# A long-convolution block with a token-mixing MLP: work of the second layer norms moved from VectorE to GpSimd and ScalarE

## The chip, the cores and the metric

The kernel runs on one core of a Trainium2 chip. A core has TensorE (matrix products into PSUM), VectorE, ScalarE and GpSimd (elementwise work), and SyncE, whose queue issues most of the DMAs. Each engine takes its instructions in the order in which the program lists them; semaphores make one engine wait for another. The time is the device time of one execution in microseconds (us). Before the change it is 712.46 us, the median of three runs (706.91, 712.46 and 717.07).

In the profile, PE is TensorE, PEld its weight loads, DVE is VectorE, ACT is ScalarE, POOL is GpSimd and SP is SyncE. L60 is line 60 of the kernel; as all plain two-operand operations go through one helper on that line, they are told apart by their tiles.

## The reference

All tensors are float32; there are S = 2048 tokens, D = 640 channels and F = 1728 hidden units.

```
mod = silu(c) @ w_mod                      -> sa, ca, ga, sb, cb, gb   (640 each)
h   = layernorm(q) * (1 + ca) + sa
kv  = conv4(k, shift_k) * v                (causal, 4 taps, by channel)
y   = longconv(kv, ssm_k) + kv * ssm_D     (causal, 2048 taps, by channel; an FFT)
x   = q + ga * (h * y)
h2  = layernorm(x) * (1 + cb) + sb
u   = gelu(layernorm(h2)^T @ w1 + b1)      (over tokens: 640 x 1728)
out = x + gb * (u @ w2 + b2)^T
```

There are two layer norms in a row after the convolution: one over x, then, after scale and shift, one inside the MLP. Both are over the 640 channels of one token.

## The kernel before

The work has three stages. The first (to about 300 us) does the convolution by channel groups of 128 (NC = 5), with the Fourier transforms as matrix products (`step1`, `f2`, `i2`, `i1`). The third (from about 381 us) does the MLP: `w1` in 14 blocks of hidden units, then `w2`. The change lies between them and at the end of the first.

**Rows and pairs.** After the convolution the 2048 tokens lie as 16 rows `j` of 128 tokens by 640 channels, rows 0 to 7 in the tile `xa`, 8 to 15 in `xb`. They are handled in eight pairs `pr`. For a pair, the steps are:

- `gate` (L310) multiplies the convolution's result from PSUM by the gate, and adds it to x. For the last channel group it is called in parts: rows 0 and 1, rows 2 to 7, and rows 8 to 15 (`half` 1).
- `x1_stats` (L681), mean and variance of a row, on VectorE.
- `root_in` and `root` (L699, L710): 1/sqrt(variance + eps). GpSimd adds eps to the variance, ScalarE takes the square root, and VectorE makes it exact in a Newton step of four small instructions (`newton`, L326), the third of which multiplies by the variance plus eps. The list `roots` tells which rows' first norms and which rows' second norms share one root; there are nine, 0 to 8.
- `norm1` (L720), the first norm, on ScalarE.
- `second` (L724): VectorE multiplies by `CB` (1 + cb), sums, and adds `SB`; ScalarE squares and sums for the variance of the second norm.
- `halves` and `rests` (L740, L744): ScalarE writes the normalised row rounded to the matrix engine's format (the high part), VectorE writes what is left (the rest). They come one root later.
- `products` (L749): three matrix products (high by high, weight's rest by high, high by rest) for each row and block of hidden units, into four PSUM accumulators `acc[0..3]`: the first four blocks of the MLP.

**Weights.** A block of `w1` is split in the same way. For the first four blocks this is done by groups of four rows: `split_rows` (L416) makes the high parts on ScalarE (L419) and the rests on VectorE, one instruction of 128 x 512 for each block. Groups 0 and 1 are split at the end of the convolution (blocks 0, 1 and 3, and block 2 a little later, when its buffer is free), groups 2 and 3 in the loop over pairs, the high parts in pass 3 and 5, the rests in pass 4 and 6. From block 4 on `split_w` (L423) does whole blocks, in two buffers that blocks 0 and 1 leave.

**Modulation rows.** `mod_row` (L360) spreads a row of 640 numbers over the partitions by a product with ones into PSUM; `CB` is copied from there with 1 added (L380, VectorE), `SB` by ScalarE (L378).

**After the products.** `u_evac` (L844) applies gelu to an accumulator on ScalarE and splits it into high part and rest (ScalarE, VectorE). Four PSUM slots go round: block 4 takes the slot of `acc[0]`, so its products wait for `u_evac(0)`. ScalarE's first gelu loads another function table (at L847 in the profile).

The order on each engine is written out by hand; there is no scheduler. What stands in the text of the program first is issued first on its engine. GpSimd's queue holds, before the change, only the gate and convolution work of the first stage and then the small additions of `root_in`.

Of the kernel before, what the change touches and what calls it, by code (L numbers as in the profile page):

```python
# [10 lines left out]
F32R = mybir.dt.float32r  # L11
AF = mybir.ActivationFunctionType
ALU = mybir.AluOpType

S, D, F = 2048, 640, 1728
DC = 128
NC = D // DC
EPS = 1e-5
# [32 lines left out]
def mixer_kernel(ctx: ExitStack, tc: tile.TileContext, q, k, v, shift_k, ssm_k, ssm_D, w1, b1, w2, b2, c,  # L51
# [11 lines left out]
    def mem(tag, n, name=None):  # L63

        return sb.tile([128, n], F32, name=name or tag, tag=tag, bufs=1)
# [244 lines left out]
    def gate(c, ps, half, eng=pool, j0=0, j1=8, then=()):  # L310
        a = A1[:, 8 * half + j0:8 * half + j1]
        av = a.rearrange("p j (m e) -> p e j m", e=2)
        TT(dve, av, ps.rearrange("p (e j m) -> p e j m", e=2, j=8)[:, :, j0:j1], av, ALU.mult)
        for f_ in then:
            f_()
        x = XH[half][:, j0:j1, DC * c:DC * c + DC]
        TT(eng, x, x, a, ALU.add)
# [8 lines left out]
    def newton(r, t, v, n=None):  # L326

        dve.reciprocal(r, t)
        dve.scalar_tensor_tensor(t, r, -0.5, r, op0=ALU.mult, op1=ALU.mult)
        TT(dve, t, t, v, ALU.mult)  # L330
        dve.scalar_tensor_tensor(r, t, 1.5, r, op0=ALU.add, op1=ALU.mult)
# [28 lines left out]
    def mod_row(i, t, slot=None, later=False):  # L360

        ps, j = psum(slot).rearrange("p (h m) -> p h m", h=2), i % 3
        for h in range(2):
            pe.matmul(ps[:, h, 0:320], ones[32 * j:32 * j + 1, 0:1].to_broadcast([1, 128]),
                      t[32 * j:32 * j + 1, 320 * h:320 * h + 320], start=True, stop=True)
        ps = ps[:, :, 0:320]
        two = lambda t: t.rearrange("p (h m) -> p h m", h=2)
        if later:
            return lambda: act.activation(two(GB), ps, AF.Copy)
        if i == 0:  # L370
            act.activation(two(G0), ps, AF.Copy)
        elif i == 1:
            act.activation(two(G1), ps, AF.Copy, bias=1.0)
        elif i == 2:
            TT(dve, two(G0), ps, two(G0), ALU.mult)
            TT(dve, two(G1), ps, two(G1), ALU.mult)
        elif i == 3:
            act.activation(two(SB), ps, AF.Copy, accum_out=msb)  # L378
        elif i == 4:
            dve.tensor_scalar(two(CB), ps, 1.0, None, op0=ALU.add)  # L380


    NF, NW = 14, 4
# [12 lines left out]
    def load_w(i, t=X):  # L396
        if i >= NF + NW:
            return
        if i < NF:
            t = j16(t)  # L400
            for b in range(2):
                sync.dma_start(t[64 * b:64 * b + 64],
                               dram(w1, 16 * b * F + fo(i), [[32 * F, 64], [F, 16], [1, 128]]))
            raw[i] = (t, [slice(0, 8), slice(8, 16)])
        else:
            t = f14(t)
            load_w2(t, i - NF, 0, 14)
            raw[i] = (t, [slice(0, 7), slice(7, 14)])
# [7 lines left out]
    def split_rows(r, t, blocks, hi=True, lo=True):  # L416
        j, t = slice(4 * r, 4 * r + 4), t.rearrange("p (j m) -> p j m", j=4)
        for f in blocks if hi else ():
            act.activation(blk[f][0][:, j].bitcast(F32R), t[:, :, 128 * f:128 * f + 128], AF.Copy)  # L419
        for f in blocks if lo else ():  # L420
            TT(dve, blk[f][1][:, j].bitcast(F32R), t[:, :, 128 * f:128 * f + 128], blk[f][0][:, j], ALU.subtract)

    def split_w(i, t2=None, eng=dve):  # L423
        if i >= NF + NW:
            return
        if t2 is None:
            t2 = T_wb[i % 2]
        view = j16 if i < NF else f14
        hi, lo = view(t2[:, 0:2048]), view(t2[:, 2048:4096])
        t, parts = raw.pop(i)  # L430
        for f in parts:
            act.activation(hi[:, f].bitcast(F32R), t[:, f], AF.Copy)
        for f in parts:
            TT(eng, lo[:, f].bitcast(F32R), t[:, f], hi[:, f], ALU.subtract)
        blk[i] = hi, lo
# [243 lines left out]
    acc = []  # L679
# [4 lines left out]
            dve.bn_aggr(mv[:, j, :], bst[:, j])  # L684


    V_, T_, R_ = (T_kt[:, o:o + 32] for o in (1280, 1312, 1344))
    place = {}
    roots = (((), (0, 1)), ((0, 1), (2, 3)), ((2, 3), (4, 5)), ((4, 5), (6, 7, 8, 9)), ((6, 7), (10, 11)),
             ((8, 9), (12, 13)), ((10, 11), (14, 15)), ((12, 13), ()), ((14, 15), ()))  # L690
# [8 lines left out]
    def root_in(n):  # L699

        second_, first_ = roots[n]
        o = start[n]
        if second_:
            pool.tensor_scalar(V_[:, o:o + 2], V_[:, o:o + 2], 1 / D, EPS, op0=ALU.mult, op1=ALU.add)
            o += 2
        if first_:
            pool.tensor_scalar(V_[:, o:start[n + 1]], mv[:, first_[0]:first_[-1] + 1, 1], EPS, None, op0=ALU.add)
        act.activation(T_[:, start[n]:start[n + 1]], V_[:, start[n]:start[n + 1]], AF.Sqrt)

    def root(n):  # L710

        o = slice(start[n], start[n + 1])
        newton(R_[:, o], T_[:, o], V_[:, o])
        first_ = roots[n][1]
        if first_:
            f = slice(first_[0], first_[-1] + 1)
            dve.scalar_tensor_tensor(nm1[:, f], mv[:, f, 0], -1.0, R_[:, start[n + 1] - len(first_):start[n + 1]],
                                     op0=ALU.mult, op1=ALU.mult)

    def norm1(pr):  # L720
        for j in (2 * pr, 2 * pr + 1):
            act.activation(row(j), XR(j), AF.Identity, scale=at(R_, 1, j), bias=nm1[:, j:j + 1])
# [17 lines left out]
    def halves(pr):  # L740
        for j in (2 * pr, 2 * pr + 1):
            act.activation(H[j][0].bitcast(F32R), row(j), AF.Identity, scale=at(R_, 2, j))

    def rests(pr):  # L744
        for j in (2 * pr, 2 * pr + 1):
            dve.scalar_tensor_tensor(H[j][1].bitcast(F32R), row(j), at(R_, 2, j), H[j][0], op0=ALU.mult,
                                     op1=ALU.subtract)
# [46 lines left out]
    products(0, range(3))  # L794
    x1_stats(range(4, 6))
    second(1)
    gate(NC - 1, ps, 1, dve, then=(lambda: root_in(2), lambda: root(2), lambda: halves(1), lambda: norm1(2)))
    spill(NC - 1, (1,))
    products(0, [3])
    rests(1)  # L800
# [10 lines left out]
    for pr in range(3, 8):  # L811
        second(pr)
        if pr > 3:
            rests(pr - 1)
            products(pr - 1)
        if pr in (4, 6):
            split_rows(pr // 2, X if pr == 4 else P, range(4), False, True)
        if pr < 6:
            x1_stats(range(2 * pr + 4, 2 * pr + 6))
        root_in(pr + 1)  # L820
        root(pr + 1)
        halves(pr)
        if pr < 6:
            norm1(pr + 2)
        if pr in (3, 5):
            split_rows(pr // 2 + 1, X if pr == 3 else P, range(4), True, False)
        if pr == 4:
            load_w(4)
    rests(7)
    products(7)  # L830

# [60 lines left out]
        rest(3, a)  # L892

    T_wb = [mem("w0", 4096, "wb0b"), mem("w1", 4096, "wb1b")]
    split_w(4)
    load_w(5)
    for f_ in range(4):
        u_evac(f_, acc[f_])
    for f_ in range(4, NF):
        ps = psum().rearrange("p (h m) -> p h m", h=2)  # L900
# [213 lines left out]
```

## Time and profile before

| what | us |
|---|---|
| median of three runs | 712.46 |
| lowest and highest run | 706.91, 717.07 |
| span of the profiled execution, first to last instruction | 705.8 |
| TensorE busy in it | 644.5 (91%) |
| VectorE busy | 492.5 (70%) |
| ScalarE busy | 307.1 (44%) |
| GpSimd busy | 155.9 (22%) |

The profiled execution's own time is known as its span; the profile gives no figure for what lies around it, and the lowest of the three runs is 1.1 us above that span. The busy share is a mean over stages with different limits. In the stretch from 299 to 381 us, where the change lies, the timeline by engine tells more: in its rows stand the start, the length, the engine, the line, the operation, the tiles and their size, how many were put together, and in brackets how long the engine had been idle and which instruction ended that. The chain of waits goes back from the last instruction to whatever released each step.

### The profile page before, as it was taken

The page shows a single profiled execution, that of the slowest core. Times are in us where ns is not written, and L with a number is a line of the kernel's source. Part 1 is how long each engine was busy: PE and PEld are TensorE (multiplying, and loading weights), DVE is VectorE, ACT ScalarE, POOL GpSimd, SP SyncE. Part 2 cuts the span into 40 slices and gives each one's busy share as a digit, 9 for nine tenths or more (in the row PEclk, how much of TensorE's full clock was granted, in tenths as well). Part 3 has the DMA queues.
Part 4 walks back from the last instruction along what each step waited for, and adds up shares of the span by engine and source line. Part 5 has one row for each costly group of instructions (what it writes and reads, how often), then busy time and mean ns, then how long its engine had stood idle before and what let it go on. Part 6 is the DMA issues. An engine that isn't in the chain of part 4 may idle for free.

```text
span 705.8 us, 20785 instructions
## 1 busy us (share of the span) xinstructions
PE 644.5 (91%) x9131; PEld 624.2 (88%) x9131; DVE 492.5 (70%) x861; ACT 307.1 (44%) x473; POOL 155.9 (22%) x135
## 2 busy tenths in 40 slices
PE   0699779989999989977899999999999999999997
PEld 0699469889999989777899999999999999999997
DVE  7778468969879638888884312311298979888886
ACT  0664554645745645556767223222334322333331
POOL 5297039615526428100010000000000000000000
PEclk9999979999999999999999999999999999999999
DMA  9968978446333522361303543354163243555511
GB/s 180 219 205 238 350 148 168 110 76 144 68 62 88 172 59 68 115 150 30 60 1 60 99 82 60 61 103 77 52 194 105 88 149 99 166 170 170 148 60 38
DMA packets 166672, 82.80 MB, mean 117 GB/s; under 512 B 89235, under 2 KB 157622, under 8 KB 166582
## 3 DMA queue, kind: packets, MB, share of 16 engines
q1 hardware_dynamic: 162034, 80.17, 46.0%
q10 hardware_dynamic: 4548, 1.31, 1.1%
q8 instruction: 71, 1.16, 0.7%
q14 instruction: 19, 0.16, 0.1%
HBM read 70.97 MB, written 10.49 MB: 115 GB/s over the span
## 4 chain that ended last, share of the span: by engine, by line
PE 65%; DVE 16%; ACT 4%; DMA 4%; POOL 4%; issue 3%; SPq 2%; ACTq 0%; DVEq 0%; POOLq 0%
PE pst L443 21%; PE pst L974 17%; PE pst L1051 7%; PE pst L229 7%; PE pst L245 6%; PE pst L274 4%; POOL y L60 3%; DVE tap L60 3%; PE pst L293 2%; DVE kt L60 2%; DVE p L60 2%; DMA aux<-in_w_mod_dram 2%; SPq L163 2%; DVE aux L60 1%; DVE y L60 1%
## 5 line engine op out<-in xcount | busy, mean ns | idle before, releaser
L245 PEld LDWEIGHTS pst<-z,w 128*64 128x64 f32 x2560 | 94.6, 141 | 7.9 <-ACT z L231 7.3
L245 PE MATMUL pst<-z,w 128*64 128x64 f32 x2560 | 95.8, 240 | 6.2 <-ACT z L231 6.1
L60 POOL TENSOR_TENSOR y<-p 128x256 f32<-128x256 f32 x72 | 92.3, 1341 | 22.4 <-DVE p L60 21.9
L60 DVE TENSOR_TENSOR p<-pst,kt 128x512 f32<-128x512 f32 x80 | 52.4, 691 | 23.8 <-ACT kt L249 15.5
L229 PE MATMUL pst<-v,x 128*64 128x128 f32 x640 | 44.3, 297 | 23.6 <-DVE x L60 23.6
L231 ACT ACTIVATE z<-pst 128x1024 f32<-128x1024 f32 x40 | 45.9, 1148 | 42.7 <-PE pst L229 23.1
L229 PEld LDWEIGHTS pst<-v,x 128*64 128x64 f32 x640 | 42.5, 220 | 24.1 <-POOL t L468 23.5
L847 ACT ACTIVATE pst<-pst,sm 128x640 f32<-128x640 f32 x14 | 10.7, 767 | 85.7 <-PE pst L443 85.7
L249 ACT ACTIVATE kt<-pst 128x512 f32<-128x512 f32 x40 | 25.1, 627 | 47.4 <-PE pst L245 26.6
L274 PEld LDWEIGHTS pst<-v,y 32*128 32x128 f32 x1280 | 38.1, 187 | 6.7 <-POOL y L60 3.8
L229 PE MATMUL pst<-v,p 128*64 128x128 f32 x640 | 39.6, 282 | 4.2 <-issue 2.2
L274 PE MATMUL pst<-v,y 32*128 32x64 f32 x1280 | 40.0, 272 | 3.8 <-DVE y L60 2.7
L974 PE MATMUL pst<-r_z,m_w 128*128 128x320 f32 x222 | 41.6, 309 | 0.7 <-DVE m_w L60 0.7
L229 PEld LDWEIGHTS pst<-v,p 128*64 128x64 f32 x640 | 36.9, 142 | 5.6 <-issue 2.9
L962 ACT ACTIVATE m_w<-m_v 128x896 fp32r<-128x896 f32 x24 | 22.2, 949 | 38.5 <-DVE m_v L60 23.1
L60 DVE TENSOR_TENSOR tap<-tap,kt 128x512 f32<-128x512 f32 x51 | 35.6, 698 | 1.3
L60 DVE TENSOR_TENSOR kt<-in,tap 128x512 f32<-128x512 f32 x51 | 35.0, 686 | 1.5
L974 PEld LDWEIGHTS pst<-r_z,m_w 128*128 128x128 f32 x222 | 34.8, 188 | 0.9 <-DVE m_w L60 0.9
L60 DVE TENSOR_TENSOR m_w<-m_v,m_w 128x896 fp32r<-128x896 f32 x24 | 26.0, 1088 | 9.5 <-ACT m_w L962 9.5
L282 ACT ACTIVATE z<-pst 128x512 f32<-128x512 f32 x38 | 21.5, 670 | 23.2 <-PE pst L274 23.2
L962 ACT ACTIVATE m_w<-m_p 128x896 fp32r<-128x896 f32 x12 | 11.5, 954 | 41.2 <-DVE m_p L60 24.4
L443 PE MATMUL pst<-r_z,wb0b 128*128 128x320 f32 x180 | 28.1, 310 | 0.9 <-DVE u_x L60 0.9
(278 smaller groups left out, 1436.9 us busy)
## 6 DMA issues: line engine op xcount, KB each, us to landing
x<-in_B_w_dram SPq DMA_DIRECT2D x22, 512.0 KB
m_v<-in_B_w_dram SPq DMA_DIRECT2D x15, 384.0 KB
x<-in_B_w_dram SPq DMA_DIRECT2D x14, 384.0 KB
aux<-in_A_ssm_k_dram SPq DMA_DIRECT2D x10, 512.0 KB
in<-in_A_k_dram SPq DMA_DIRECT2D x36, 128.0 KB
in<-in_A_v_dram SPq DMA_DIRECT2D x36, 128.0 KB
m_x<-xs SPq DMA_DIRECT2D x28, 160.0 KB
out_dram<-m_x SPq DMA_DIRECT2D x28, 160.0 KB
```

What stands on the lines that cost most here:

```text
L60: TT = lambda eng, o, a, b, op: eng.tensor_tensor(o, a, b, op=op)
L163: sync.dma_start(KSR[64 * h:64 * h + 64].rearrange("p (i n) -> p i n", i=64), dram(ssm_k, (DC * c + 64 * h) * S, [[32, 64], [S, 64], [1, 3 ...
L229: pe.matmul(ps[64 * ri:64 * ri + 64, o:o + 128], lhs, F1[:, 128 * ri:128 * ri + 128], start=True, stop=True)
L231: evac = lambda: act.activation(Z[:, side, t].rearrange("p a k e -> p e a k"), ps.rearrange("p (e a k) -> p e a k", a=8, e=2), AF.Copy)
L245: pe.matmul(ps[64 * h:64 * h + 64, o:o + 64], W2[k1 // 32][:, 2 * (k1 % 32) + ri], rhs, start=True, stop=True)
L249: act.activation(kt.rearrange("p (m i) -> p m i", i=32), pv[:, :, 1], AF.Copy)
L274: pe.matmul(pp[qd // 2][:, o:o + 64], Y[p, ri, i:i + 2].rearrange("p i k -> p (i k)"), V2[p, 64 * ri:64 * ri + 64], start=ri == 0, stop=ri ...
L282: act.activation(o, i, AF.Copy)
L443: pe.matmul(ps[0:m, h, 0:320], w_.bitcast(F32R), r_[:, 320 * h:320 * h + 320].bitcast(F32R), start=first and i == 0, stop=last and i == 2)
L962: act.activation(W[n][0].bitcast(F32R), A[p, w_], AF.Copy)
L974: pe.matmul(bank[n], w[:, i].bitcast(F32R), r.bitcast(F32R), start=i == 0 and k == 0, stop=i == 6 and k == 2)
L1051: pe.matmul(acc[s][:, h, 0:320], w[:, f_].bitcast(F32R), u[r + h].bitcast(F32R), start=f_ == 0 and k == 0, stop=f_ == NF - 1 and k == 2)
```

## The change

Five things:

1. `split_rows` writes the weights' rests on GpSimd instead of VectorE (16 instructions of 128 x 512). Groups 2 and 3 now have high parts and rests in the same pass, 3 and 5; the call in passes 4 and 6 goes. On GpSimd's queue the rests stand ahead of the additions of the roots that follow.
2. `root_in` takes the square root on ScalarE straight from the variance (and from the sum of squares, scaled), with eps as bias; GpSimd's addition goes to another place (`VE`), which only the third Newton instruction reads. A root that serves first and second norms takes two instructions on ScalarE instead of one.
3. `CB` is copied out of PSUM by ScalarE.
4. The addition of the last gate (rows 8 to 15, 128 x 1024) goes from VectorE to GpSimd; there it stands behind the additions of root 2.
5. A gelu on one column, whose result nothing uses, stands ahead of the last rests, so that the function table is loaded there; and `u_evac(0)` comes ahead of the split of block 4.

```diff
@@ mod_row
         elif i == 4:
-            dve.tensor_scalar(two(CB), ps, 1.0, None, op0=ALU.add)
+            act.activation(two(CB), ps, AF.Copy, bias=1.0)
@@ split_rows
         for f in blocks if lo else ():
-            TT(dve, blk[f][1][:, j].bitcast(F32R), t[:, :, 128 * f:128 * f + 128], blk[f][0][:, j], ALU.subtract)
+            TT(pool, blk[f][1][:, j].bitcast(F32R), t[:, :, 128 * f:128 * f + 128], blk[f][0][:, j], ALU.subtract)
@@ root_in, root
-    V_, T_, R_ = (T_kt[:, o:o + 32] for o in (1280, 1312, 1344))
+    V_, T_, R_, VE = (T_kt[:, o:o + 32] for o in (1280, 1312, 1344, 1376))
...
         o = start[n]
+        if first_:
+            f, v = slice(o + len(second_), start[n + 1]), mv[:, first_[0]:first_[-1] + 1, 1]
+            act.activation(T_[:, f], v, AF.Sqrt, bias=epsc)
+            pool.tensor_scalar(VE[:, f], v, EPS, None, op0=ALU.add)
         if second_:
-            pool.tensor_scalar(V_[:, o:o + 2], V_[:, o:o + 2], 1 / D, EPS, op0=ALU.mult, op1=ALU.add)
-            o += 2
-        if first_:
-            pool.tensor_scalar(V_[:, o:start[n + 1]], mv[:, first_[0]:first_[-1] + 1, 1], EPS, None, op0=ALU.add)
-        act.activation(T_[:, start[n]:start[n + 1]], V_[:, start[n]:start[n + 1]], AF.Sqrt)
+            act.activation(T_[:, o:o + 2], V_[:, o:o + 2], AF.Sqrt, scale=1 / D, bias=epsc)
+            pool.tensor_scalar(VE[:, o:o + 2], V_[:, o:o + 2], 1 / D, EPS, op0=ALU.mult, op1=ALU.add)
...
-        newton(R_[:, o], T_[:, o], V_[:, o])
+        newton(R_[:, o], T_[:, o], VE[:, o])
@@ the order of the second norms
-    gate(NC - 1, ps, 1, dve, then=(lambda: root_in(2), lambda: root(2), lambda: halves(1), lambda: norm1(2)))
+    gate(NC - 1, ps, 1, then=(lambda: root_in(2), lambda: root(2), lambda: halves(1), lambda: norm1(2)))
...
-        if pr in (4, 6):
-            split_rows(pr // 2, X if pr == 4 else P, range(4), False, True)
...
         if pr in (3, 5):
-            split_rows(pr // 2 + 1, X if pr == 3 else P, range(4), True, False)
+            split_rows(pr // 2 + 1, X if pr == 3 else P, range(4))
         if pr == 4:
             load_w(4)
+    act.activation(tm[:, 0:1], epsc, AF.Gelu_apprx_tanh)
     rests(7)
     products(7)
@@ after the products
+    u_evac(0, acc[0])
     split_w(4)
     load_w(5)
-    for f_ in range(4):
+    for f_ in range(1, 4):
         u_evac(f_, acc[f_])
```

In `gate` the default engine of the addition is GpSimd.

## The prediction

> **What bounds the kernel now.** First the page: which engine fills the span, and which carries the chain that ended last.
>
> ```profile
> span 705.8 us, 20785 instructions
> PE 644.5 (91%) x9131; PEld 624.2 (88%) x9131; DVE 492.5 (70%) x861; ACT 307.1 (44%) x473; POOL 155.9 (22%) x135
> PE 65%; DVE 16%; ACT 4%; DMA 4%; POOL 4%; issue 3%; SPq 2%; ACTq 0%; DVEq 0%; POOLq 0%
> ```
>
> TensorE is busy for 91% of the span. The change touches only some 95 us in the middle, so I read the chain in order of time from there on (start, length, what).
>
> ```profile
> 365.81 9.06 PE pst L443 x60
> ...
> 376.93 1.28 ACT L847
> 378.22 0.78 ACT pst L847
> ...
> 381.03 141.06 PE pst L443 x960
> ```
>
> From 381.03 to 522.1 the chain is TensorE alone, on one line: whatever moves that start moves the end by as much. Before 365.81 the same chain goes through VectorE, ScalarE and GpSimd in turns. So the account is one date, the start of block 4 at 381.03, and the timeline of TensorE tells what sets it (start, length; in brackets the idle time before and who ended it).
>
> ```profile
> 318.53 2.02 PE L443 MATMUL pst<-r_z,wb 128*128 128x320 f32 x12 [1.71 <-DVE aux L60]
> ...
> 330.61 8.72 PE L443 MATMUL pst<-r_v,wb 128*128 128x320 f32 x48 [2.48 <-ACT r_v L742]
> ...
> 365.81 14.33 PE L443 MATMUL pst<-h_x,wb 128*128 128x320 f32 x96 [0.57 <-ACT h_x L742]
> 381.03 2.90 PE L443 MATMUL pst<-r_z,wb0b 128*128 128x320 f32 x18 [0.90 <-DVE u_x L60]
> ```
>
> The last 96 products of the first four blocks wait for root 7, and then run through by themselves to 365.81 + 14.33 = 380.14. Block 4 follows 0.90 later, when the first gelu has emptied its accumulator. So two dates count: root 7, and those 0.90 us. Root 8 counts only if it slips by more than the products have in hand.
>
> **The port.** Much of the change moves work from VectorE to GpSimd. The timelines of the two engines show what happens when both read operands from SBUF: first VectorE, then GpSimd.
>
> ```profile
> 79.33 0.50 DVE L60 TENSOR_TENSOR sm<-sm 128x16 f32<-128x16 f32 x1
> ...
> 93.86 2.49 DVE L60 TENSOR_TENSOR aux<-aux,g 128x1024 f32<-128x1024 f32 x2
> ...
> 99.17 3.45 DVE L60 TENSOR_TENSOR aux<-aux,g 128x1024 f32<-128x1024 f32 x2 [1.49 <-ACT aux L300]
> ...
> 319.72 0.16 DVE L331 SCALAR_TENSOR_TENSOR kt<-kt 128x4 f32<-128x4 f32 x1
> ```
>
> ```profile
> 79.17 1.09 POOL L594 TENSOR_SCALAR t<-rows 128x256 f32<-128x256 f32 x1
> ...
> 99.52 4.23 POOL L60 TENSOR_TENSOR t<-in,t 128x512 f32<-128x512 f32 x2 [19.27 <-DMA in<-in_A_k_dram]
> 103.83 1.27 POOL L60 TENSOR_TENSOR t<-t 128x512 f32<-128x512 f32 x1
> ...
> 151.57 2.38 POOL L60 TENSOR_TENSOR xa<-xa,aux 128x1024 f32<-128x1024 f32 x1 [16.11 <-DVE aux L60]
> ...
> 267.26 17.96 POOL L60 TENSOR_TENSOR y<-p 128x256 f32<-128x256 f32 x14 [6.96 <-DVE p L60]
> ...
> 308.74 0.19 POOL L704 TENSOR_SCALAR kt<-kt 128x2 f32<-128x2 f32 x1 [7.76 <-ACT r_z L738]
> 309.01 0.22 POOL L707 TENSOR_SCALAR kt<-sm 128x2 f32<-128x2 f32 x1
> ...
> 345.13 0.91 POOL L704 TENSOR_SCALAR kt<-kt 128x2 f32<-128x2 f32 x1 [7.94 <-ACT r_z L738]
> ```
>
> At 99 us two GpSimd operations take 4.23 instead of 2 x 1.27, and VectorE's pair beside them 3.45 instead of 2.49: they take turns. The tiny GpSimd step grows from 0.19 to 0.91 when VectorE's weight rests run, and a small VectorE step (128x16) needs 0.50 beside a GpSimd step that starts at 79.17, where such steps take 0.16 with GpSimd idle (128x4, at 319.72). So I count GpSimd's and VectorE's two-operand work in SBUF as one queue. The Trainium skill says the same in "SBUF — State Buffer", section "Who interferes with whom": a VectorE instruction with two SBUF inputs contends with a GpSimd instruction that reads SBUF, and whichever holds the shared pair blocks the other for its whole instruction. The trace agrees on the turns (3.45 for 2.49), though not on the whole instruction: VectorE got through at 79.83, before GpSimd's 1.09 was over at 80.26. By the page alone this change would move no work off the shared path.
>
> **The change part by part**, each as its shift of root 7 or of block 4 (minus is earlier). What VectorE loses, and between it the copies that it owes at 295.05 and the last Newton steps of roots 5 and 7 (L331; that of root 2 stands above at 319.72):
>
> ```profile
> 295.05 1.29 DVE L280 TENSOR_SCALAR z<-pst 128x512 f32<-128x512 f32 x2 [0.42 <-PE pst L274]
> ...
> 303.18 0.82 DVE L380 TENSOR_SCALAR kt<-pst 128x640 f32<-128x640 f32 x1
> ...
> 320.00 1.22 DVE L60 TENSOR_TENSOR xb<-xb,aux 128x1024 f32<-128x1024 f32 x1
> ...
> 343.49 2.50 DVE L60 TENSOR_TENSOR wb<-x,wb 128x512 fp32r<-128x512 f32 x4
> ...
> 348.24 0.16 DVE L331 SCALAR_TENSOR_TENSOR kt<-kt 128x4 f32<-128x4 f32 x1
> ...
> 361.25 2.50 DVE L60 TENSOR_TENSOR wb<-p,wb 128x512 fp32r<-128x512 f32 x4
> ...
> 364.73 0.16 DVE L331 SCALAR_TENSOR_TENSOR kt<-kt 128x2 f32<-128x2 f32 x1
> ```
>
> ScalarE's rows: the norms, a root, the high parts, the first split and the end of the first evacuation.
>
> ```profile
> 302.43 1.73 ACT L722 ACTIVATE t_g<-xa,sm,kt 128x640 f32<-128x640 f32 x2 [1.22 <-DVE sm L717]
> ...
> 309.26 0.21 ACT L708 ACTIVATE kt<-kt 128x4 f32<-128x4 f32 x1 [0.60 <-POOL kt L707]
> ...
> 341.43 2.18 ACT L419 ACTIVATE wb<-x 128x512 fp32r<-128x512 f32 x4
> ...
> 359.20 2.18 ACT L419 ACTIVATE wb<-p 128x512 fp32r<-128x512 f32 x4
> ...
> 374.89 2.01 ACT L432 ACTIVATE wb0b<-x 128x1024 fp32r<-128x1024 f32 x2 [2.21 <-PE pst L443]
> ...
> 380.02 0.44 ACT L853 ACTIVATE u_x<-pst 128x320 fp32r<-128x320 f32 x1 [0.56 <-DVE u_t L60]
> ```
>
> (a) *First eight rests.* On VectorE they lay beside TensorE's inverse transform and cost nothing: VectorE still waited 0.42 for it at 295.05. On GpSimd they are 8 x 1.27 = 10.2 us from 267.26 + 17.96 = 285.2 on, and VectorE's four steps of 128x1024 (2.49 / 2 each, as at 93.86), which start about 1 us later, must share with six of them. With a turn of 1.0 to 1.27 lost at each, they end at 286.2 + 5.0 + 4.0 to 5.1 = 295.2 to 296.3, 0.1 to 1.2 after VectorE is wanted; without any turn, nothing is lost. The last two rests run to about 299.4, beside the first small gate addition. Bounds 0 to +1.2; I take **+0.3**, near the row with the idle 0.42.
>
> (b) *The row to ScalarE.* VectorE loses 0.75 (0.82 less the overlap with its neighbour). ScalarE has 1.22 idle before its layer-norm rows (302.43), where the copy fits; the rows come as before and the next multiplication can start with the first of them: **-0.75**.
>
> (c) *Roots.* Before, a root goes from ScalarE's square through two GpSimd steps to ScalarE's root (308.74, 309.01, then 309.26). ScalarE waited 0.60 for GpSimd; instead it now does a second root of 0.21, about half of it overlapped. That gives 0.3 at root 1, some 0.5 at root 2, and 0.15 to 0.2 at roots 3, 4 and 6, where the statistics come last and only one GpSimd step of about 0.25 went, less the added root. GpSimd's addition now runs beside, but VectorE's third Newton step waits for it, so the gain holds only while GpSimd's queue is empty. Through root 1: **-0.3**, which with (a) and (b) makes -0.75.
>
> (d) *The gate's addition to GpSimd.* It is issued behind root 2's additions, starts as soon as VectorE has multiplied, at 318.5 - 0.75 = 317.8, and holds the port for most of its 2.38. VectorE stands before the small Newton steps of root 2, all with two SBUF operands. They end at about 320.5 instead of 319.9, the halves of ScalarE behind them too, and the 1.14 that VectorE saves is lost. Cumulated: from -0.75 to **+0.5**. If GpSimd did not hold the small steps, this step would be 1.14 + 0.5 earlier: -2.0 instead.
>
> (e) *Roots 3 and 4*: -0.25, cumulated **+0.3**.
>
> (f) *Four rests at root 5.* VectorE loses 4 x 0.60 = 2.41. But GpSimd's four are queued ahead of both additions of root 5. The first high part (a quarter of 2.18 after 341.43) is ready at 342.0 + 0.3; four at 1.2 spacing make 4.8, a turn of VectorE's rests between them 0.8; so they end near 348.0. Two small additions, 0.5, and the last Newton steps, 0.4: root 5 ends at 348.9 instead of 348.4. Cumulated **+0.5**: the whole 2.41 is gone.
>
> (g) *Root 6* -0.15, then *four rests at root 7.* First high part at 359.20 + 0.6 + 0.4 = 360.2; one or two turns of VectorE's rests, 0.8 to 1.6; four rests 4.9; so 365.9 to 366.7, and 0.7 for the addition and the rest of Newton: 366.6 to 367.4 against 364.9. I take the lower end, less what the rests of the two engines overlap at their edges: **+1.9**. What was queued behind: VectorE's second(7), which has slack against the products.
>
> (h) *First gelu sooner.* The table load of 1.28 moves into ScalarE's 2.21 of waiting before 374.89, and the first evacuation comes ahead of the split. From 378.22 to 380.46 the evacuation took ScalarE 2.24; the split then ends at 374.89 + 2.24 + 2.01 = 379.1, and VectorE's first half near 379.4, before TensorE is through at 380.14. So all of the 0.90 goes: **-0.9**. DMA order is the same; the load of rows 8 to 11 waits for GpSimd, with over 35 us in hand.
>
> **Sum: +1.9 - 0.9 = +1.0 us**, block 4 at 382.0, a span of 706.8. The profiled span of 705.8 is 1.1 below the lowest run (706.91) and 6.7 below the median; I add the shift to the median: 712.46 + 1.0 = **713.5**.
>
> **Rivals.**
> *No sharing.* If the rests run beside VectorE's work, (a) is 0, (b) to (e) give -2.1, at root 5 GpSimd's own 4.8 still replaces 2.41 (-2.7), root 7 comes to -2.4, and with (h) it is -3.3: 709.2. For it: GpSimd's operation at 103.83 took its plain 1.27 beside VectorE at work. Against: the pair at 99 us. Chance 0.2.
> *Slower by a cold clock.* Where TensorE idles long enough, its clock halves. Granted clock is the number after TensorE's, VectorE's, ScalarE's and GpSimd's busy times:
>
> ```profile
> 316.00:324.00 8.00, 6.04 (x40) 5.51 (x39) 7.22 (x14) 5.01 (x9) 0.41 (x2) 1.00 0.18 39
> 328.00:336.00 8.00, 5.52 (x28) 5.39 (x28) 6.40 (x17) 6.02 (x10) 0.24 (x1) 0.79 0.00 1
> 346.00:356.00 10.00, 7.23 (x39) 6.97 (x38) 8.27 (x26) 5.03 (x10) 1.05 (x4) 0.83 0.56 105
> 365.00:381.00 16.00, 14.57 (x98) 14.07 (x96) 10.56 (x19) 10.35 (x16) 0.70 (x1) 1.00 0.05 12
> ```
>
> A gap of 1.71 left it at 1.00; around one of 2.48 it lost 0.21 x 8 = 1.7 us, a stretch of 3.4 at half clock. The last 96 products ran at 1.00 after a gap of 0.57. Root 7 later by 1.9 makes that gap up to 2.5; from a point between 1.71 and 2.48 on it costs 1.7 on the path: +2.7, 715.2. With one more GpSimd turn (1.2) ahead of root 7, 716.4. Against it: a half clock in blocks of products before it, as at 346, would fill the gap. The Trainium skill, "TensorE: Matmul & The Clock Gate", Part 1, gives the window as 3.4 us and free-running, so a gap shorter than a window would count or not by its phase; the trace agrees in the length (3.4). Chance 0.25.
> *The gelu gains nothing*, because the evacuation or the split ends after the products: +1.9, 714.4. Chance 0.1. The forecast itself has 0.45.
>
> **The numbers.** All cases lie within 709.2 to 716.4, but three runs of one kernel spread over 706.91 to 717.07, and a median of few runs moves by some 3 us, more than the cases differ; so the range is 707 to 718.5. Two per cent, about what a measurement of this kernel tells from no change, is 14 us, more than any case: faster 0.01, same 0.96, slower 0.03.
>
> **What would show it.** Right: 128x512 rests on GpSimd well over 1.27, VectorE's small Newton steps of root 2 stretched to about 2 us, Newton of roots 5 and 7 waiting for GpSimd, block 4 directly behind the products. Wrong: rests at 1.27 and unstretched VectorE beside them, or root 7 before 364. A stall that I do not see, of a load or of the loop behind 381, would break the forecast altogether.

## The result, and the profile after

The changed kernel took 718.31 us in the median of 20 runs (711.01 to 726.98), the kernel before 709.79 in 20 runs beside it (703.62 to 723.14). The ratio is 1.0102, with a 95% interval of 1.0081 to 1.0122: no change by the measure of two per cent, but some 7 us slower, where the forecast said 1.0 slower. Measured a second time (with the third profile below), it took 712.64 against 708.78: 1.0042, interval 1.0009 to 1.0074, or 3.0 us. The ratios here leave out the slowest executions, those over 1.5% above the fastest of their kernel, so they differ from the quotients of the medians, and the profiled execution of the changed kernel, 725.44 us, is one of those left out. The two intervals don't overlap, so the changed kernel's time is not one number, and the forecast shift of 1.0 us lies in the second interval only. The reason for both has to be found.

First the page of the changed kernel.

```profile
span 723.7 us, 20797 instructions
PE 656.6 (91%) x9131; PEld 635.1 (88%) x9131; DVE 493.6 (68%) x843; ACT 308.9 (43%) x481; POOL 178.8 (25%) x152
PE 67%; DVE 16%; POOL 7%; ACT 3%; DMA 3%; issue 3%; ACTq 0%; DVEq 0%; SPq 0%; POOLq 0%
```

GpSimd's busy time has grown by 22.9 and its share of the chain from 4% to 7%. VectorE's busy time has not fallen at all (492.5 before), although it has 18 instructions fewer (861 before): the time of what it no longer does has come back as longer instructions. Where it stands is told by the chain in order of time (start, length, what), at the end of the convolution and at root 5 and 7.

```profile
283.41 8.75 DVE y L60
...
292.30 7.18 PE pst L274 x128
...
358.41 6.21 POOL wb L60 x4
...
377.06 6.15 POOL wb L60 x4
```

Two things stand out. The four rests on GpSimd are now on the chain at root 5 and at root 7, as forecast. And one addition into Y on VectorE takes 8.75 us. The timelines show what lies beside it: first VectorE, then GpSimd, then TensorE.

```profile
283.33 9.33 DVE L60 TENSOR_TENSOR y<-p 128x256 f32<-128x256 f32 x2
```

```profile
279.89 4.48 POOL L60 TENSOR_TENSOR y<-p 128x256 f32<-128x256 f32 x4
284.34 3.70 POOL L60 TENSOR_TENSOR wb<-x,wb 128x512 fp32r<-128x512 f32 x3
288.00 3.69 POOL L60 TENSOR_TENSOR wb<-aux,wb 128x512 fp32r<-128x512 f32 x3
```

```profile
292.30 7.18 PE L274 MATMUL pst<-v,y 32*128 32x64 f32 x128 [7.61 <-DVE y L60]
...
301.70 7.11 PE L274 MATMUL pst<-v,y 32*128 32x64 f32 x128
...
311.02 3.32 PE L293 MATMUL pst<-z,v 64*64 64x64 f32 x128
```

The first six weight rests ran on GpSimd back to back at 3.70 / 3 = 1.23 each, not slowed at all, and VectorE's addition, which had started at 283.33 beside GpSimd's last one, came through only when the sixth was over. There were no turns: seven GpSimd instructions passed before VectorE, and at the six ends between them it did not get in. This is called the shut-out below; that the addition stood at the port all that time, and did not last for some other reason that the trace draws as busy time, is the reading that fits the rests beside it, and no run shows it by itself. TensorE, which needs Y, was idle for 7.61, and worked at a granted clock of 0.50 afterwards (7.18, where the same 128 products took 4.10 before). L293, the first product of the last inverse step, starts at 311.02.

For the kernel before, the same view has:

```profile
282.09 2.35 PE L353 MATMUL tap<-in,sm 128*32 128x320 f32 x24
...
285.85 4.10 PE L274 MATMUL pst<-v,y 32*128 32x64 f32 x128 [0.32 <-ACT wb L419]
...
296.48 2.10 PE L293 MATMUL pst<-z,v 64*64 64x64 f32 x128 [0.28 <-DVE z L280]
...
349.32 3.44 PE L443 MATMUL pst<-h_a,wb 128*128 128x320 f32 x16 [2.77 <-ACT h_a L742]
```

And VectorE's timeline of the kernel before has, for the two additions into Y and the four multiplications behind them:

```profile
284.17 2.05 DVE L60 TENSOR_TENSOR y<-p 128x256 f32<-128x256 f32 x2
...
289.76 4.87 DVE L60 TENSOR_TENSOR aux<-aux,g 128x1024 f32<-128x1024 f32 x4
```

So L293 came 14.5 us later in this execution, or 15.4 counted from L353, which starts 0.8 earlier here: 7.3 of idle time, and 8.1 of a half clock. That is more than the median shows, and it may be a chance of this execution. The experiments below therefore look at the changed kernel again, and take the change apart.

### The profile page after: what moved, and what is told of

Read it like the earlier page. It is cut to its first block, busy times and chain, and to the rows that moved or that the text cites. A ratio compares the mean times of both kernels' runs of the same rounds, so it can differ in the third digit from the quotient of the medians.

```text
span 723.7 us, 20797 instructions
## 1 busy us (share of the span) xinstructions
PE 656.6 (91%) x9131; PEld 635.1 (88%) x9131; DVE 493.6 (68%) x843; ACT 308.9 (43%) x481; POOL 178.8 (25%) x152
## 4 chain that ended last, share of the span: by engine, by line
PE 67%; DVE 16%; POOL 7%; ACT 3%; DMA 3%; issue 3%; ACTq 0%; DVEq 0%; SPq 0%; POOLq 0%
PE pst L443 21%; PE pst L975 17%; PE pst L229 7%; PE pst L1052 7%; PE pst L274 6%; PE pst L245 5%; POOL y L60 4%; DVE tap L60 3%; DVE kt L60 2%; DVE y L60 2%; DMA aux<-in_A_ssm_k_dram 2%; POOL wb L60 2%; PE pst L293 2%; DVE p L60 2%; PE tap L353 1%
## 5 line engine op out<-in xcount | busy, mean ns | idle before, releaser
L274 PEld LDWEIGHTS pst<-v,y 32*128 32x128 f32 x1280 | 45.7, 220 | 13.4 <-POOL wb L60 8.2
L274 PE MATMUL pst<-v,y 32*128 32x64 f32 x1280 | 47.7, 307 | 10.0 <-DVE y L60 9.3
L293 PEld LDWEIGHTS pst<-z,v 64*64 64x64 f32 x1280 | 23.7, 153 | 5.6 <-issue 2.7
```

The lines of the kernel that those rows point to most:

```text
L274: pe.matmul(pp[qd // 2][:, o:o + 64], Y[p, ri, i:i + 2].rearrange("p i k -> p (i k)"), V2[p, 64 * ri:64 * ri + 64], start=ri == 0, stop=ri ...
L293: pe.matmul(ps[64 * b:64 * b + 64, 512 * e + 64 * jj:512 * e + 64 * jj + 64], V1[p, ri, n2], T2[p, :, 32 * ri + n2], start=ri == 0, stop=r ...
```

## Experiments

**The first eight rests back on VectorE.**

```
-            TT(pool, blk[f][1][:, j]..., t[:, :, 128 * f:128 * f + 128], blk[f][0][:, j], ALU.subtract)
+            TT(dve if r < 2 else pool, blk[f][1][:, j]..., t[:, :, 128 * f:128 * f + 128], ...)
```

> The changed kernel with the first eight weight rests (row groups 0 and 1) on VectorE again; all else of the change stays. Theory 'shut out' (the six back-to-back rests keep VectorE's addition after the transform, 8.8 us instead of 0.6, out of the port; TensorE idles 7.6 and comes back at half clock): the addition takes 0.6 to 1.5, TensorE's inverse transform starts at 285 to 286 instead of 292.3, and the kernel comes back by about 7 us, to between 0 and +2 us against the kernel before. Rival 'turns' (the wait of that addition is a chance of one run, the loss lies in the later steps that the prediction named): it stays at +5 to +7 us against the kernel before.

Measured: 710.61 against 708.88, ratio 1.0029 (0.9984 to 1.0075), about 2 us, at the upper end of what was expected if the shut-out carries the loss; the interval reaches into what the rival expected. In the profile L274 starts at 285.72, as in the kernel before. But this was measured on another chip than the second measurement of the whole change, whose 1.0042 is no different from 1.0029 within the intervals; so it doesn't show that the eight rests carry the 1.0102. What stays is roots 5 and 7. In this profile the last 96 products, and block 4 behind them, stand so on TensorE's timeline:

```profile
368.43 15.88 PE L443 MATMUL pst<-h_x,wb 128*128 128x320 f32 x96 [2.33 <-ACT h_x L743]
384.14 2.80 PE L443 MATMUL pst<-r_z,wb0b 128*128 128x320 f32 x18
```

They start 2.62 later than before and took 15.88 instead of 14.33, behind a gap of 2.33: half a clock for some 3 us, the rival of the cold clock, at its place.

**The first eight rests alone, on the kernel before.**

```
-            TT(dve, blk[f][1][:, j]..., t[:, :, 128 * f:128 * f + 128], blk[f][0][:, j], ALU.subtract)
+            TT(pool if r < 2 else dve, blk[f][1][:, j]..., t[:, :, 128 * f:128 * f + 128], ...)
```

> The kernel before with only the first eight rests moved to GpSimd. 'Shut out': it alone is slower than the kernel before by +6 to +8 us, nearly the whole loss of the change. 'Turns': 0 to +1.2 us, as the prediction's step (a) has it.

Measured: 712.94 against the same 708.88, ratio 1.0033 (0.9993 to 1.0074), about 2.3 us: more than turns were expected to cost, and far less than the shut-out. In its profile there are turns and no shut-out. VectorE's timeline:

```profile
284.38 3.05 DVE L60 TENSOR_TENSOR y<-p 128x256 f32<-128x256 f32 x2
287.35 8.93 DVE L60 TENSOR_TENSOR aux<-aux,g 128x1024 f32<-128x1024 f32 x4
```

The two additions into Y, which took 9.33 above, take 3.05 here (2.05 in the kernel before), and the four multiplications take 8.93 instead of 4.87. On TensorE's timeline that is 1.0 us from L353 to L293.

**The rests set apart.** Behind each of the first eight rests, GpSimd makes a 128x1 step that reads its last value, so that they no longer follow one another directly.

```
             TT(pool, blk[f][1][:, j]..., t[:, :, 128 * f:128 * f + 128], blk[f][0][:, j], ALU.subtract)
+            if r < 2:
+                pool.tensor_scalar(tm[:, f:f + 1], blk[f][1][:, 4 * r + 3, 127:128], 1.0, None, op0=ALU.mult)
```

> The changed kernel with a tiny GpSimd step (128x1, reads the last column of the rest, so that it waits for it) behind each of the first eight rests. Same work, but GpSimd's queue no longer holds two rests that can follow each other without a gap. 'Shut out' by the missing gap: VectorE's addition gets in after one rest, 1.5 to 2.5 us instead of 8.8, and the kernel gains 4 to 7 us on the changed one. Rival 'first come holds until its work is done whatever the gaps' (or the addition waits for something else): it stays at about 8 us and the time stays that of the changed kernel.

Measured: 715.0, ratio 1.0082 (1.0045 to 1.0120). In the profile VectorE got in after the first rest, as was expected of the gap, if a little later (2.9 us for the first addition instead of 1.5 to 2.5), but the 4 to 7 us that were expected with it were not won:

```profile
287.68 3.45 DVE L60 TENSOR_TENSOR y<-p 128x256 f32<-128x256 f32 x2
291.04 8.16 DVE L60 TENSOR_TENSOR aux<-aux,g 128x1024 f32<-128x1024 f32 x4
```

VectorE is through with both in 11.5, no later than with plain turns (11.9 in the kernel just above). What TensorE loses here is in part half clock: L274 took 5.95, and the granted clock was 0.59 and 0.56 in the two stretches of 4 us from 292 on. So a time nearly as long as that of the first measurement came with a profile in which VectorE did not wait beyond the first rest.

**Without any rest and without the gate on GpSimd**: only the row on ScalarE, the new roots and the first gelu sooner. Of the change, the diff to the kernel before keeps L380, `root_in`, `root`, the early gelu and `u_evac(0, acc[0])`; `split_rows`, the call of `gate` and the loop's split stay as they were.

> The changed kernel with all sixteen rests and the gate's addition on VectorE as before: only the row on ScalarE, the roots behind ScalarE alone and the first gelu sooner are left. Both theories: these three are free of the port, -0.75 for the row, -0.3 to -0.5 at roots 1 and 2, -0.15 at roots 3 to 6, up to -0.9 at roots 7 and 8 where GpSimd's small step waited beside VectorE, and -0.9 for the gelu: -2.5 to -3.5 us against the kernel before, about 0.4%. If the row or the roots cost something that the traces do not show, it is 0 or above.

> The same kernel as e4_no_rests_no_gate, measured more closely: only the CB row on ScalarE, the new roots and the first gelu sooner, while all weight rests and the gate's addition stay on VectorE. By the prediction's (b), (c) and (h), -0.75 and -0.9 with little added: -1.5 to -2.5 us, 0.9965 to 0.998. If the new roots or the gelu cost something that the other parts hid, 0.999 to 1.002.

Measured: 707.07, ratio 0.9972 (0.9939 to 1.0004), and, in a second measurement on another chip, 705.90 against 708.78, ratio **0.9953 (0.9915 to 0.9991)**. The first gain is less than was expected, the second a little more. This kernel is faster than both, though by less than the two per cent that count as a change. TensorE's timeline of the second run:

```profile
302.27 2.10 PE L293 MATMUL pst<-z,v 64*64 64x64 f32 x128 [0.28 <-DVE z L280]
...
316.18 5.57 PE L443 MATMUL pst<-r_z,wb 128*128 128x320 f32 x36 [0.20 <-ACT r_z L743]
...
335.06 8.86 PE L443 MATMUL pst<-r_v,wb 128*128 128x320 f32 x48 [2.43 <-ACT r_v L743]
...
369.65 14.35 PE L443 MATMUL pst<-h_x,wb 128*128 128x320 f32 x96 [1.07 <-ACT h_x L743]
383.83 2.36 PE L443 MATMUL pst<-r_z,wb0b 128*128 128x320 f32 x15
```

From L293 to block 4 it takes 81.56 instead of 381.03 - 296.48 = 84.55: 3.0 less. (Its convolution happened to end later, which is why the dates themselves are late.)

**The last eight rests alone, on the kernel before**: groups 2 and 3 on GpSimd in pass 3 and 5.

```
-            TT(dve, blk[f][1][:, j]..., t[:, :, 128 * f:128 * f + 128], blk[f][0][:, j], ALU.subtract)
+            TT(dve if r < 2 else pool, blk[f][1][:, j]..., t[:, :, 128 * f:128 * f + 128], ...)
...
-        if pr in (4, 6):
-            split_rows(pr // 2, X if pr == 4 else P, range(4), False, True)
...
-            split_rows(pr // 2 + 1, X if pr == 3 else P, range(4), True, False)
+            split_rows(pr // 2 + 1, X if pr == 3 else P, range(4))
```

> The kernel before with one part alone: the rests of w1's last two groups of rows (four in pass 3, four in pass 5) on GpSimd instead of VectorE. By the prediction's steps (f) and (g) the gains of 2.41 and 0.4 on VectorE are eaten by Newton steps that wait for GpSimd: +1 to +4 us, 1.001 to 1.005. Without sharing, VectorE gets 2.4 to 2.8 us back on the path: 0.996 to 0.997. If these eight carry the lost time, 1.007 or more.

Measured: 713.71 against 709.80, ratio 1.0053 (1.0013 to 1.0092), or 3.8 us slower, within what the prediction's steps lead to and far from a gain. TensorE's timeline:

```profile
296.17 2.10 PE L293 MATMUL pst<-z,v 64*64 64x64 f32 x128 [0.28 <-DVE z L280]
...
350.50 4.11 PE L443 MATMUL pst<-h_a,wb 128*128 128x320 f32 x16 [4.29 <-ACT h_a L742]
...
369.50 15.86 PE L443 MATMUL pst<-h_x,wb 128*128 128x320 f32 x96 [3.11 <-ACT h_x L742]
386.25 2.91 PE L443 MATMUL pst<-r_z,wb0b 128*128 128x320 f32 x18 [0.89 <-DVE u_x L60]
```

Counted from L293, root 5 costs 1.5 (350.50 against 349.32, less the 0.31 that L293 is earlier), root 7 brings it to 4.0, and a half clock behind the gap of 3.11 adds 1.5. These eight rests take 2.41 twice off VectorE, and the kernel is slower for it.

**The first eight rests held back until Y is done.** A 128x1 step on GpSimd, ahead of them, reads the last value that VectorE adds into Y.

```
+            pool.tensor_scalar(tm[:, 15:16], Y[:, 1, 0, 63:64], 1.0, None, op0=ALU.mult)
             split_rows(0, X, (0, 1, 3))
```

> The changed kernel with a 128x1 GpSimd step ahead of the first eight rests that reads the last value VectorE adds into Y, so that none of the rests can run before VectorE is done with Y; the rests then run beside the four 1.2 us multiplications aux<-aux,g instead. If the shut-out of that addition is what the forecast lacked, the time comes down to between 1.002 and 1.005 of the kernel before (710 to 713), as when these eight rests go back to VectorE. If the lost time lies in the sharing of the later steps, in roots 5 and 7, or in the multiplications, it stays at 1.008 to 1.012.

Measured: 711.54 against 709.80, ratio 1.0009 (0.9972 to 1.0047), below what was expected: with the wait for Y, what the eight rests cost is no longer to be seen in the time. The interval overlaps with that of the second measurement of the whole change, so how much the wait gains is not settled by the times. VectorE's timeline shows the two additions nearly as in the kernel before (2.05 there), TensorE's that L274 waits only 0.48, and the busy times by stretch a granted clock of 0.50 from 293 to 298, with TensorE busy throughout:

```profile
284.11 2.22 DVE L60 TENSOR_TENSOR y<-p 128x256 f32<-128x256 f32 x2
```

```profile
285.95 4.99 PE L274 MATMUL pst<-v,y 32*128 32x64 f32 x128 [0.48 <-DVE y L60]
290.86 2.36 PE L353 MATMUL tap<-z,sm 128*32 128x320 f32 x12
293.15 7.11 PE L274 MATMUL pst<-v,y 32*128 32x64 f32 x128
```

```profile
293.00:298.00 5.00, 5.00 (x95) 4.85 (x92) 0.15 (x1) 0.13 (x1) 4.96 (x4) 0.50 0.01 3
```

This execution was the longest of its ten (715.69), and it shows something else: L353 at 2.36 and L274 at 7.11 are half clock, for over 10 us, behind a gap of 0.48 only. The first profile of the kernel without any rest on GpSimd has the same, a granted clock of 0.50 from 296 to 308. So in the first profile of the changed kernel, too, the half clock behind 292 need not come from the 7.61 of idle time, nor from the rests.

**The changed kernel again**, unchanged, three more profiles.

> The changed kernel unchanged, a second profile. If the shut-out of VectorE's last addition into Y behind the first six rests is regular, the addition takes 8 to 9 us again and TensorE idles over 7 us ahead of L274; if it is a race that is lost now and then, the addition may take 0.6 to 2.5 us and L274 then starts some 6 to 8 us sooner against the start of L353.

> The changed kernel once more, a third profile and a second measurement beside the next kernel: 1.008 to 1.012 of the kernel before. VectorE's first addition into Y behind the rests was 8.82 and 3.90 us long in the first two looks; if how long it is shut out differs from run to run, it will be another length here, between 0.6 and 9 us, and the run's time should follow it.

> A fourth profile of the changed kernel, for the same question: the length of that addition, and of the one behind it.

The single execution of the second profile took 720.03; with the third came the second measurement (712.64, as told above, less than the 1.008 to 1.012 that were expected), its own execution at 709.79; that of the fourth took 708.19. VectorE's timelines of profile 2 and then profile 3 have for the two additions into Y:

```profile
286.53 5.49 DVE L60 TENSOR_TENSOR y<-p 128x256 f32<-128x256 f32 x2
```

```profile
283.38 3.01 DVE L60 TENSOR_TENSOR y<-p 128x256 f32<-128x256 f32 x2
286.32 8.92 DVE L60 TENSOR_TENSOR aux<-aux,g 128x1024 f32<-128x1024 f32 x4
```

Profile 4 has 3.04. So they took 9.33, 5.49, 3.01 and 3.04 in the four profiles, with spans of 723.7, 718.2, 708.0 and 706.4: the same program is shut out for long, for less, or not at all. The spans go the same way, but not by the shut-out alone. The second is 10.2 longer than the third: 3.2 of it was there when L353 started (284.46 against 281.30), 2.5 is the longer additions, and 4.4 is half clock on the products behind them. Profile 2 was made on one chip, profiles 3 and 4 on another, so it may hang on the chip as well as on the moment.

**The dispute by itself.** Two kernels with thirty trials each behind the work of the kernel before (their own times mean nothing). In the first, GpSimd makes six subtractions of 128x512, and VectorE a step that reads PSUM, of ten lengths, and then one step with two SBUF operands. In the second, the order of the real place is repeated:

```
+            for r in range(2):
+                TT(pool, y_(2 + r), t_[:, 0], t_[:, 1], ALU.subtract)
+            for i in range(6):
+                TT(pool, TC[:, 512 * i:512 * i + 512]..., TA[:, 0:512], ..., ALU.subtract)
+            TT(dve, TC[:, 7168:7168 + n], pt[:, 0:n], TA[:, 0:n], ALU.mult)
+            for r in range(2):
+                TT(dve, TE[:, 512 * r:512 * r + 512], pt[:, 0:512], TA[:, 0:512], ALU.mult)
+            TT(dve, y_(0), t_[:, 0], t_[:, 1], ALU.subtract)
```

> The kernel before, with thirty trials behind its work (its own time means nothing, it is over 100 us longer). In each trial ScalarE releases both engines, GpSimd runs six subtractions of 128x512, and VectorE a step that reads PSUM, of 32 to 608 columns, and then one step with two SBUF operands: the strided 128x256 addition or a plain 128x512 subtraction. In ten trials of each of the first two kinds the six are independent of each other, in ten each reads the output of the one before it. Theory A (a run of independent GpSimd steps can shut VectorE out for several steps): some or all of the independent trials show a VectorE step of over 2.5 us, up to the rest of the run of six (some 7 us), and the dependent ones none over 2. Theory B (turns; the 8.82 us step was something else, such as a wait for a semaphore that the trace draws as busy time): VectorE waits at most one GpSimd step in all thirty, so no step above 0.7 + 1.3 = 2.0 us.

> The kernel before with thirty other trials behind its work, closer to the place: GpSimd runs two strided 128x256 additions and then six 128x512 subtractions; VectorE a leading PSUM step of 32 to 464 columns, two PSUM multiplications of 128x512 and then two strided 128x256 additions that read what these two wrote. In the second ten ScalarE writes 128x512 conversions that the six wait for, in the third ten VectorE's additions read other, older data. If the shut-out is made by these two engines' own order of steps, some of the first ten show an addition of over 2.0 us; if it needs ScalarE's writes, only the second ten do; if by reading its own fresh result, the first and second but not the third. If none does, what makes it is something that the trials lack, and it stays open.

The groups of VectorE's additions in the two (nanoseconds, shortest, median and longest; first and last start):

```profile
L60 DVE TENSOR_TENSOR tr_y<-tr_p x30: 579/1362/1744, 720.3 to 964.6; 128x256 f32<-128x256 f32 x20, 128x512 f32<-128x512 f32 x10
```

```profile
L60 DVE TENSOR_TENSOR tr_y<-tr_p x60: 978/1575/1660, 726.4 to 1035.3; 128x256 f32<-128x256 f32 x60
```

In ninety steps VectorE never waited for more than one GpSimd instruction. So a run of independent GpSimd steps does not shut VectorE out as a rule, nor do ScalarE's writes or the fresh operand, which the trials varied. But each set of trials is one execution, and the second was made on the chip on which profiles 3 and 4 show no shut-out either; something that differs from one execution to the next is not refuted by them. What makes the shut-out stays open.

## Why the prediction was right and wrong

Where there were turns (profiles 3 and 4 of the changed kernel), the account can be checked step by step. TensorE's timeline of profile 3:

```profile
281.30 2.35 PE L353 MATMUL tap<-in,sm 128*32 128x320 f32 x24
...
296.65 2.10 PE L293 MATMUL pst<-z,v 64*64 64x64 f32 x128 [0.28 <-DVE z L280]
...
310.56 5.56 PE L443 MATMUL pst<-r_z,wb 128*128 128x320 f32 x36 [1.73 <-ACT r_z L743]
...
331.10 7.33 PE L443 MATMUL pst<-r_v,wb 128*128 128x320 f32 x48 [2.12 <-ACT r_v L743]
...
350.90 4.15 PE L443 MATMUL pst<-h_a,wb 128*128 128x320 f32 x16 [3.66 <-ACT h_a L743]
...
369.16 14.34 PE L443 MATMUL pst<-h_x,wb 128*128 128x320 f32 x96 [2.34 <-ACT h_x L743]
383.34 2.80 PE L443 MATMUL pst<-r_z,wb0b 128*128 128x320 f32 x18
```

The stage begins 0.79 earlier than before (L353), by chance of the execution; everything below is counted from there.

| date on TensorE | before | profile 3 | shift + 0.79 | forecast |
|---|---|---|---|---|
| L293, step (a) | 296.48 | 296.65 | +0.96 | +0.3 |
| first products, (b) and (c) | 311.26 | 310.56 | +0.09 | -0.75 |
| products behind root 3, (d) and half of (e) | 330.61 | 331.10 | +1.28 | +0.4 |
| products of root 5, (f) | 349.32 | 350.90 | +2.37 | +0.5 |
| last products, (g) | 365.81 | 369.16 | +4.14 | +1.9 |
| block 4, (h) | 381.03 | 383.34 | +3.10 | +1.0 |

The sum in turns is 3.1 us, which agrees with the second measurement's 3.0. Of the 2.1 us by which it misses the forecast, (f) is 1.0, (a) 0.7 and (g) 0.4.

The kernel without rests and gate on GpSimd tells the price of each move. Its distances from L293 to the first products and from the last products to block 4 are those of profile 3 (13.91 and 14.18); between them they differ by what is on GpSimd. From the first products to those behind root 3 it is 18.88 there and 20.54 in profile 3, so the gate's addition, which was given no kernel of its own, costs 1.7. From there to the last products it is 34.59 and 38.06: 3.5 for the last eight rests. The first eight cost 1.1 by L293. These 6.2, less the 3.1 that the other parts gain against the kernel before (counted from L353), are the sum.

- **(a) failed.** It counted the four multiplications of 128x1024, and they took 8.92, just under its 9.0 to 10.1. But it started them where they would start if nothing had touched VectorE before. The two additions into Y right ahead of them also read two SBUF operands and also stand beside the first rests: 3.01 with turns, 2.05 before. TensorE's L274 waits for them, and the multiplications start later by as much. So (a) came to 0.66 more than the value taken, still inside the bounds of 0 to 1.2. When VectorE is shut out, the same two take up to 9.33, and the bounds, which allow one turn lost at each of the four multiplications, are broken. What the first measurement's 7 us are made of beyond the 3 of the turns stays open. The shut-out was seen in two executions, of 725.44 and 720.03 us, and more than half of what the first of them lost by L293 was half clock, which came without a shut-out in other kernels. How many of the 20 runs were shut out, and for how long, no profile tells; only one of them was seen.
- **(b), (c)**: -0.87 between the first two rows of the table, forecast -1.05. Right.
- **(d) with root 3**: +1.19, forecast +1.15. Right. VectorE's small Newton step beside the gate's addition, on the timelines of VectorE and GpSimd of profile 3:

```profile
318.12 2.15 DVE L329 SCALAR_TENSOR_TENSOR kt<-kt 128x4 f32<-128x4 f32 x1
...
349.62 0.16 DVE L60 TENSOR_TENSOR kt<-kt 128x4 f32<-128x4 f32 x1 [1.80 <-POOL kt L709]
```

```profile
317.86 2.39 POOL L60 TENSOR_TENSOR xb<-xb,aux 128x1024 f32<-128x1024 f32 x1
...
342.81 6.21 POOL L60 TENSOR_TENSOR wb<-x,wb 128x512 fp32r<-128x512 f32 x4 [4.99 <-ACT wb L419]
...
361.46 6.12 POOL L60 TENSOR_TENSOR wb<-p,wb 128x512 fp32r<-128x512 f32 x4 [4.64 <-ACT wb L419]
```

- **(f), with root 4, had the mechanism, but the size was off.** Newton of root 5 waits for GpSimd, as the prediction said: VectorE's third step at 349.62 stands behind 1.80 of waiting for it. But the four rests took 6.21 instead of 5.6, since VectorE's two rests took a turn each and not one between them, and they began at 342.81, or 343.60 counted as in the table, instead of 342.3; 0.9 of that had been brought along from the steps before. From root 3 to root 5 it cost 1.1 instead of 0.1. The kernel with these eight alone shows 1.5 at the same place.
- **(g)**: +1.77, forecast +1.4: the four rests took 6.12 instead of 4.9 + 0.8. The forecast's own dates add up to less than it wrote: 366.6 - 364.9 is 1.7, and not +1.9, before anything is taken off for an overlap.
- **(h)**: -1.04, forecast -0.9. Block 4 stands directly at the products' end, and ScalarE's timeline of profile 3 has the table load in front of the first gelu, as said:

```profile
375.64 1.28 ACT L828 ACT_TABLE_LOAD   x1
...
378.25 0.77 ACT L847 ACTIVATE pst<-pst,sm 128x640 f32<-128x640 f32 x1 [1.11 <-PE pst L443]
```

Of the rivals, *no sharing* is refuted: the late rests alone make the kernel slower by 3.8, not faster. (Its figure of -2.0 behind (d) does not follow either: -0.75 less 1.14 + 0.5 is -2.4.) *The gelu gains nothing* is refuted by (h). *The cold clock* is real, but did not decide where the prediction had it: behind a gap of 2.34 the last products ran at full clock (14.34, profile 3), and behind one of 2.33 they lost 1.55 (15.88, the first eight on VectorE). At the end of the convolution, where the prediction had no term for it, it cost 8.1 us in the first profile. That gaps of one length go both ways is what the Trainium skill, "TensorE: Matmul & The Clock Gate", Part 1, leads one to expect from a free-running window; its lower limit for a loss, one idle window of about 3.4 us, the traces don't bear out, for 2.33 was enough.

The range of 707 to 718.5 held both medians. It was made wide for the scatter of the runs, not for a shut-out, which no case of the prediction had; 718.31 lies at its edge, and that it lies inside is luck. So is the nearness of 713.5 to the second median of 712.64: the forecast added its shift to 712.46, a median of three runs, and the kernel before has 709.79 and 708.78 in the larger sets, from where +1.0 leads to 710.8 and 709.8. What was right is the direction, the turns with GpSimd, and the steps at which they cost time; the shift was three times as large in turns, and some seven times in the first measurement.

The page that the prediction cited in favour of sharing, the Trainium skill's "SBUF — State Buffer", says in its section "SBUF: two separate sides" that whichever of the two instructions starts first gets the shared pair for the whole instruction. The ninety steps of the trials agree: none waited longer than one GpSimd instruction. That the waiting engine loses several ends in a row, six in the first profile, does not follow from it, and no trial here brought it about.

## What to carry to other kernels

Moving two-operand steps from VectorE to GpSimd won no time here while both read SBUF, and what suffers is not only the step that was moved: look for every two-operand step of VectorE that will stand beside it, the short ones that TensorE waits for above all. Here the half of the change that took small waits out of the path (a row to ScalarE, roots without GpSimd in front, an early gelu) gained 0.5%, and the half that moved work between the two engines cost more than that. If such work has to go to GpSimd, let it wait for the step that the path needs, as with Y, rather than hope for a turn: the two additions then took 2.22, though the times do not settle what that was worth. And a single execution is a weak witness: L353, ahead of the change, started anywhere from 279.67 to 284.46 in the four profiles of the changed kernel.

## What was not expected of the hardware

- VectorE's two 128x256 additions took 9.33 us in one execution, since seven GpSimd instructions in a row passed ahead of the first, the six rests among them at 1.23 each as if alone; in other executions of the same program the two took 5.49 or 3.0. The cause was not found.
- TensorE ran at half clock for over 10 us behind a gap of only 0.48 (the rests held back until Y is done), busy all the while, and at full clock behind one of 2.34.
